# A fused cosine attention and highway layer: q in quads of heads, k left unscaled until the exponential, and a new order of the work

## The chip, the cores and the metric

The kernel runs on one core of a Trainium2 chip. The metric is device time in microseconds (us), the median of several runs. The engines are PE (TensorE; PEld are its weight loads), DVE (VectorE), ACT (ScalarE), POOL (GpSimd) and SP, which only issues transfers here.

## The reference

```python
def _attn_ref(q, k, v, tau):                      # (8, 12, 448, 64) each, tau 0.1
    q_n = q / (np.linalg.norm(q, axis=-1, keepdims=True) + 1e-06)
    k_n = k / (np.linalg.norm(k, axis=-1, keepdims=True) + 1e-06)
    scores = np.matmul(q_n, k_n.transpose(0, 1, 3, 2)) / tau
    attn = np.exp(scores - np.max(scores, axis=-1, keepdims=True))
    attn = attn / (np.sum(attn, axis=-1, keepdims=True) + 1e-09)
    return np.matmul(attn, v)
def _moe_ref(x, w_h, w_t, b_t):                   # x: (3584, 768), w: (768, 768)
    H = np.maximum(x @ w_h, 0.0)
    T = 1.0 / (1.0 + np.exp(-(x @ w_t + b_t)))
    return T * H + (1.0 - T) * x
```

The heads' outputs stand side by side in x: 8 batches of 448 tokens, 768 wide.

## The kernel before

The work goes batch by batch (8), and in a batch by pairs of heads p and p + 6 (6 pairs). The 448 tokens of a head are three chunks of 128 (token 3 l + c on lane l) and a tail of 64.

*Loads.* `load_main` (L361) takes the three chunks of q and k of a batch with one transfer each on POOL's queue, cast to f16 on the way; `load_tails` (L389) takes the tails as f32 on SP's queue; `load_v` (L410) takes v as f32 on SP's queue. Batch 0 comes partly by `load_first` (L377).

*Norms.* `square` (L450) squares q and k on DVE in f16, `folds` (L471) adds halves twice and reduces on DVE; tails are squared on ACT (L487). `newton` (L495) makes 1/norm by two Newton steps, seven small DVE instructions a part.

*Scaling and turning.* `scaled` (L526, the instruction at L532) multiplies q and k of a pair by 1/norm on POOL, giving qn and kp; `qtnorm` (L542) does q's tails on POOL, `ktnorm` (L554, L559) k's tails on DVE into kb. `turn` (L568) transposes on PE, nine 128x128 products a pair, and DVE copies the 1,024 columns to qT (L591).

*Scores.* `scores` (L594) makes, per chunk of k, two products of 64 rows by 448 columns (L600), one for each head, into two PSUM banks, and one exponential of 896 (L607, scale 1/tau) takes both; the tails of k of both heads are one 512-wide product (L614) and exponential (L619). There is no maximum to subtract, since the scores are bounded.

*Attend.* `vcast` and `vtcast` (L623, L632) cast v to f16 on ACT; a 65th column of ones gives the sum of the exponentials. `attend` (L641) gathers 7 groups of 65 columns in one PSUM bank: L648 and L651 for full chunks, L667 for the tail tokens of both heads. DVE takes the reciprocal of the sums (L681) and writes x (L684).

*Highway layer.* `ffn` (L691) runs four times a batch: three groups of 128 tokens over 768 columns, and a tail group whose two column halves stand on the two halves of the lanes. x is transposed (L710) and copied (L715). The bias enters as a product of a row of ones with the bias (L733, tail L730), then come six products of 384 columns per weight and half (L744, tail L739). ACT takes the tanh from PSUM (L758), DVE max(h, 0) - x (L765), the gate (L772) and their product (L776), POOL adds x (L782; in the last two groups DVE), SP stores (L792, tail L790).

*The order.* All this is recorded as some 1,790 operations. The list `ORDER` (L17) puts them in a fixed order; `Plan.follow` (L187) walks the list, gives out buffers by due time and sorts by the start that its own cost figures give. Each engine executes its share in that order. PSUM is two score buffers of two banks (pS) and four banks for all else (pB).

Of the kernel before, what the change touches and what calls it, by code (L numbers as in the profile page):

```python
# [15 lines left out]

ORDER = tuple(  # L17
    int(n)
    for n in """
# [861 lines left out]
```

## Time and profile before

| what | value |
|---|---|
| median of 3 runs | 318.89 us (317.71 to 319.69) |
| span of the profiled execution, first to last instruction | 317.8 us |
| granted TensorE clock, mean | 0.974 of full speed |
| read from HBM, written | 37.75 MB, 11.01 MB |
| first transfer to first exponential of 896 | 20.6 us |
| weights w_h, w_t landed | 34.8, 42.6 us |
| last x written to the end | 25 us |

A group's row in the page reads: line, engine, operation, out<-in, shapes, count, then busy time, mean ns of one, and idle time of the engine just before with what ended it. Recorded durations of neighbours overlap, so the step from one instruction to the next is shorter than a duration. In the slices a digit is the busy share of 1/40 of the span, in tenths.

### The profile page before, as it was taken

How to read it: one execution, taken by the hardware profiler on the slowest of the kernel's cores; microseconds unless marked ns; L12 is line 12 of the kernel's file. 1: busy time of each engine (PE TensorE's matmuls, PEld its weight loads, DVE VectorE, ACT ScalarE, POOL GpSimd, SP SyncE). 2: the span in 40 equal slices, each digit the busy share in tenths (PEclk: the TensorE clock that was granted, in tenths of full speed). 3: DMA queues.
4: the chain of work that ended last, by engine and by line, in shares of the span. 5: the costliest groups of instructions: out<-in, count | busy, mean ns of one | idle time of the engine just before them, and what ended most of it. 6: DMA issues, size and time to landing. Idle time of an engine off the chain costs nothing.

```text
span 317.8 us, 8195 instructions
## 1 busy us (share of the span) xinstructions
PE 272.9 (86%) x3304; PEld 172.9 (54%) x3304; DVE 251.5 (79%) x572; ACT 206.3 (65%) x327; POOL 157.7 (50%) x162
## 2 busy tenths in 40 slices
PE   0167668999899999989999499996999999999992
PEld 0025344665566566555675366573665675666651
DVE  6697794499989987998799969997589686464554
ACT  2348675869789765967777538953699747684120
POOL 9542656243773496277544817349372637010521
PEclk9999995999999999999999989997999999999998
DMA  7999999019921399139811991228911111110304
GB/s 165 254 187 218 228 188 242 14 48 150 228 101 27 105 232 188 28 106 233 153 60 58 146 221 49 71 71 121 273 70 27 49 52 52 28 52 1 123 33 145
DMA packets 62854, 38.09 MB, mean 120 GB/s; under 512 B 43328, under 2 KB 59712, under 8 KB 62816
## 3 DMA queue, kind: packets, MB, share of 16 engines
q1 hardware_dynamic: 36208, 25.47, 29.0%
q0 software_dynamic: 24992, 11.31, 27.6%
q10 hardware_dynamic: 1616, 0.79, 0.9%
q8 instruction: 26, 0.43, 0.5%
q14 instruction: 12, 0.10, 0.1%
HBM read 37.75 MB, written 11.01 MB: 153 GB/s over the span
## 4 chain that ended last, share of the span: by engine, by line
PE 43%; DVE 28%; DMA 11%; issue 9%; POOL 4%; ACT 3%; SPq 1%; POOLq 0%; ACTq 0%; DVEq 0%
PE pB L744 17%; PE pS L600 5%; PE pB L651 4%; DMA kr<-in_k_dram 3%; PE pB L739 3%; DVE f L478 3%; DMA qr<-in_q_dram 3%; DVE sq L463 3%; PE pB L710 3%; DVE hm L765 3%; DVE f L479 2%; DVE n L480 2%; DMA f<-in_k_dram 2%; DMA qt<-in_q_dram 2%; DVE qT L591 2%
## 5 line engine op out<-in xcount | busy, mean ns | idle before, releaser
L607 ACT ACTIVATE E<-pS 128x896 f16<-128x896 f32 x144 | 126.3, 925 | 23.6 <-PE pS L600 22.7
L782 POOL TENSOR_TENSOR os<-x,hm 128x768 f32<-128x768 f16 (+1 forms) x30 | 46.5, 1554 | 84.6 <-DVE hm L776 80.8
L744 PEld LDWEIGHTS <-xT 128*128 128x128 f16 x576 | 52.1, 99 | 36.1 <-issue 10.0
L744 PE MATMUL pB<-wt,xT 128*128 128x384 f16 x288 | 62.3, 331 | 0.1
L744 PE MATMUL pB<-wh,xT 128*128 128x384 f16 x288 | 60.9, 331 | 1.0 <-DVE x L684 0.5
L758 ACT ACTIVATE tt<-pB 128x384 f16<-128x384 f32 x56 | 27.4, 496 | 45.8 <-PE pB L744 35.5
L532 POOL TENSOR_TENSOR kp<-kr,rs 128x384 f16<-128x384 f16 x45 | 40.2, 902 | 29.6 <-DVE rs L513 17.0
L651 PE MATMUL pB<-vp,E 128*128 128x65 f16 x864 | 50.6, 195 | 0.8 <-ACT E L607 0.8
L532 POOL TENSOR_TENSOR qn<-qr,rs 128x384 f16<-128x384 f16 x45 | 39.6, 891 | 22.1 <-PE pB L579 11.0
L765 DVE SCALAR_TENSOR_TENSOR hm<-pB,x 128x384 f16<-128x384 f32 x56 | 30.7, 553 | 23.6 <-PE pB L744 19.9
L600 PE MATMUL pS<-qT 64*128 64x448 f16 x288 | 45.3, 367 | 3.6 <-ACT E L607 3.2
L619 ACT ACTIVATE Et<-pB 128x512 f16<-128x512 f32 x48 | 28.8, 605 | 25.6 <-PE pB L614 22.9
L648 PE MATMUL pB<-vp,Et 128*128 128x65 f16 x288 | 43.9, 194 | 0.5 <-DVE xT L715 0.4
L651 PEld LDWEIGHTS <-E 128*128 128x128 f16 x864 | 40.1, 98 | 5.7 <-ACT E L607 1.3
L591 DVE COPY qT<-pB 128x1024 f16<-128x1024 f16 x48 | 32.3, 682 | 6.9 <-PE pB L585 5.4
L648 PEld LDWEIGHTS <-Et 128*128 128x128 f16 x288 | 28.2, 98 | 9.6 <-issue 6.6
L684 DVE SCALAR_TENSOR_TENSOR x<-pB,rd 128x448 f16<-128x448 f32 x48 | 29.5, 620 | 0.9
L614 PE MATMUL pB<-qT 128*128 128x512 f16 x48 | 19.1, 403 | 4.9 <-DVE qT L591 3.4
L600 PEld LDWEIGHTS <-qT 64*128 64x128 f16 x288 | 10.8, 94 | 21.6 <-issue 16.6
L577 PE MATMUL pB<-ident,qtn 128*128 128x128 f16 x24 | 5.7, 237 | 18.1 <-POOL qtn L545 13.8
L478 DVE TENSOR_TENSOR f<-sq 128x1152 f16<-128x1152 f16 (+2 forms) x25 | 18.4, 746 | 3.3 <-ACT sq L461 3.2
L715 DVE COPY xT<-pB 128x768 f16<-128x768 f16 (+1 forms) x32 | 15.8, 502 | 4.7 <-PE pB L710 4.6
(73 smaller groups left out, 466.1 us busy)
## 6 DMA issues: line engine op xcount, KB each, us to landing
vr<-in_v_dram SPq DMA_DIRECT2D x8, 1152.0 KB, 10.8
out_dram<-os SPq DMA_DIRECT2D x24, 384.0 KB, 2.3
qr<-in_q_dram POOLq DMA_DIRECT2D x7, 576.0 KB, 8.5
kr<-in_k_dram POOLq DMA_DIRECT2D x7, 576.0 KB, 11.6
vt<-in_v_dram SPq DMA_DIRECT2D x16, 96.0 KB, 7.7
out_dram<-os SPq DMA_DIRECT2D x16, 96.0 KB, 2.2
qt<-in_q_dram SPq DMA_DIRECT2D x30, 48.0 KB, 3.8
kt<-in_k_dram SPq DMA_DIRECT2D x14, 96.0 KB, 7.8
```

The source lines that it names most:

```text
L478: lambda: nc.vector.tensor_add(v("f1"), v("sq")[:, :, 0:32], v("sq")[:, :, 32:64]),
L532: e.tensor_mul(R("qn" if t == 0 else "kp", s).rearrange("l c ab d -> l ab c d"), rows(t, b, p, p + 1)[:, :, 0, :].rearrange("l ab (c d) -> ...
L591: op("DVE", f"cpT {s}", lambda: nc.vector.tensor_copy(R("qT", s)[:, :], R16(("T", ti))[:, :]), o, l, key, r=[("B", ("T", ti))], w=[("qT", s)])
L600: nc.tensor.matmul(R("S", 3 * s + c)[:, ab, 0:448], lhsT=qT[:, 512 + 128 * c : 640 + 128 * c], rhs=qT[:, 64 * (1 - ab) : 64 * (1 - ab) + 4 ...
L607: nc.scalar.activation(R("E", s)[:, c, :, 0:448], R("S", 3 * s + c)[:, :, 0:448], AF.Exp, scale=inv_tau)
L619: op("ACT", f"exp {s} t", lambda: nc.scalar.activation(R("Et", s)[:, 64:576], R("B", ("S", s))[:, :], AF.Exp, scale=inv_tau), o, l, key + 0.3,
L648: nc.tensor.matmul(U[:, 2 * c + ab, :], lhsT=Et[:, 128 + 128 * c : 256 + 128 * c], rhs=vp[:, 6 + ab, :], start=True, stop=False)
L651: nc.tensor.matmul(U[:, 2 * c + ab, :], lhsT=EF[:, j, 576 * ab + 128 * c : 576 * ab + 128 * c + 128], rhs=vp[:, 3 * ab + j, :], start=Fals ...
L684: op("DVE", f"ev {s}", lambda: nc.vector.scalar_tensor_tensor(out=R("x", b)[:, :, D * p : D * p + D], in0=U_()[:, :, 0:D], scalar=0.0, in1 ...
L744: nc.tensor.matmul(P[:, 0:MH], lhsT=xT[:, cc, :], rhs=w_[:, cc, MH * mh : MH * mh + MH], start=st, stop=(cc == CC - 1))
L765: nc.vector.scalar_tensor_tensor(out=R("hm", g)[:, MH * mh : MH * mh + MH], in0=R("B", ("P", pi))[:, 0:MH], scalar=0.0, in1=xs, op0=ALU.ma ...
L782: op(en, f"out {g}", lambda: eng.tensor_add(R("os", g)[:, 0:W], xall(), R("hm", g)[:, 0:W]), o, l, at + 0.1, r=[("gg", g), ("x", b)], w=[( ...
```

## The change

The kernel is rewritten in nearly all its parts, for the same tiling over batches, pairs and token groups.

- *q in quads.* q of a batch comes as f32 by two transfers on SP's queue. A lane holds seven consecutive tokens of one head; lanes 0 to 63 hold six heads, lanes 64 to 127 six others. There are no q tails. Three quads of heads a batch: each is scaled by two POOL multiplications of 448, turned by seven products, copied by DVE once (896 columns). The score products now have tokens in the order of lanes, and the groups of attend and x follow it: group j holds tokens 7 l + j.
- *k unscaled.* k is rearranged by two DVE copies a batch (`copy_k`), not multiplied; 1/|k| enters the exponential as its scale, one value per lane. tau goes into q's norm.
- *Norms.* ACT squares q (896 wide) and k (1,152 wide); DVE reduces the squares, f32, without folds. Newton runs over up to 84 columns at once.
- *Exponentials.* One per head and chunk, 448 wide, each from its own bank; 42 a batch, and none of 896 or 512.
- *Attend.* The two products with the tail of k become one of 130 columns; the tail tokens are 64-lane products of half width, eight a pair, each half on its own lanes.
- *v* is cast to f16 by its transfer on POOL's queue; DVE rearranges it; POOL casts the tails of k and v.
- *Bias.* DVE adds it to the projection (f32, into z), tanh reads z, 768 wide from SBUF.
- *PSUM* is one ring of eight single banks.
- *Order.* A new list of 1,879 operations, and `SLOTS`, which names the buffer for each use; `Plan.ordered` follows both as they stand.

Cut to its core:

```diff
-    NR = dict(qr=3, kr=3, qt=2, kt=2, ... E=3, Et=3, rd=2, x=4, xT=3, tt=3, hm=3, os=4, S=2, B=4)
+        qr=(2, [128, 6, 448], FP32), kr=(3, [128, NH, 192], FP16), kt=(2, [128, NP, D], FP32),
...
+        os=(4, [128, DM], FP32), B=(8, [128, 512], FP32))
...
+    def q_src(b, s):
+        return q[b].rearrange("(u s) (l j) d -> s l u (j d)", s=2, j=NJ)[s]
...
+            def fn(eng=eng, src=src, dst=dst):
+                if eng == "ACT":
+                    nc.scalar.activation(dst(), src(), AF.Square, scale=tau)
...
+                nc.vector.reduce_sum(R("n2", b)[:, c : c + 7 * n], s, axis=AX.X)
...
+                a = R("kr", b).rearrange("l (t p) x -> l t p x", t=2)[:, :, p0:p1]
+                nc.scalar.activation(d, a, AF.Square)
...
+                ENG[eng].tensor_mul(
+                    R("qn", 3 * b + g)[:, :, t, :],
+                    R("qr", b)[:, g + 3 * t, :].rearrange("l (j d) -> l j d", d=D),
+                    R("y", b)[:, c : c + 7].unsqueeze(2).to_broadcast([128, NJ, D]))
...
+            for j in range(NJ):
+                nc.tensor.transpose(T[:, j], R("qn", i)[:, j].rearrange("l t d -> l (t d)"), ident[:, :])
...
+    def copy_k(b):
+        for t in range(2):
+            def fn(t=t):
+                nc.vector.tensor_copy(R("kp", b).rearrange("l p c t d -> l (p c) t d")[:, :, t],
+                                      R("kr", b)[:, 6 * t : 6 * t + 6, :].rearrange("l p (c d) -> l (p c) d", c=NC))
...
-                nc.scalar.activation(R("E", s)[:, c, :, 0:448], R("S", 3 * s + c)[:, :, 0:448], AF.Exp, scale=inv_tau)
+                    nc.scalar.activation(R("E", n)[:, at : at + 7, :].rearrange("l j x -> l (j x)"), R("B", ("S", n, c, t))[:, 0:S],
+                                         AF.Exp, scale=R("y", b)[:, col : col + 1])
...
-                    nc.tensor.matmul(U[:, 6, :], lhsT=lt, rhs=rh, start=(n == 0), stop=(n == 7))
+                    lt = E[:, 7 * (2 * m + t) + 6, :] if m < NC else Et[:, 6, :]
+                    nc.tensor.matmul(U[64 * t : 64 * t + 64, 6, :], lhsT=lt, rhs=vp[:, 3 * t + m if m < NC else 6 + t, 0:65],
+                                     start=(m == 0), stop=(m == NC))
...
-                            nc.tensor.matmul(P[:, 0:MH], lhsT=ones[:, :], rhs=bth[:, MH * mh : MH * mh + MH],
-                                             start=True, stop=False)
...
-                        R("tt", g)[:, MH * mh : MH * mh + MH], R("B", ("P", pi))[:, 0:MH], AF.Tanh, scale=0.5),
+                    op("DVE", f"za {g} {mh}", lambda at=at, sl=sl: nc.vector.tensor_add(
+                        R("z", g)[:, sl], R("B", at)[:, 0:MH], biast[:, :] if tail else bias[:, sl]), r=[("B", at), ("b",)], w=[("z", g)])
+                op("ACT", f"th{nb} {g}", lambda: nc.scalar.activation(R("tt", g)[:, 0:W], R("z", g)[:, 0:W], AF.Tanh, scale=0.5),
...
-            for o in plan:
+            for o in pl.ordered(ORDER, SLOTS):
```

More of the change, by code (lines that the diff above doesn't have):

```diff
@@ L170, in begin @@
[L170 to L190 removed]
+                o.deps.update(q for q in writers[t] if q is not o)
@@ L191, in follow, with ordered @@
+    def ordered(self, order, slots):
+        self.link()
+        assert sorted(order) == list(range(len(self.ops)))
+        nth = {n: 0 for n in self.rings}
+        left, held, done = {}, {}, set()
+        for o in self.ops:
+            for t in self.buffers(o):
+                left[t] = left.get(t, 0) + 1
         out = []
-        for n in seqs:
+        for n in order:
             o = self.ops[n]
-            st, take = self.begin(o, free, mode, port)
-            for t, i in take:
-                self.held[t[0]][i] = t
-                self.slot[t] = i
-                if t[0] in self.turns:
-                    self.turns[t[0]].remove(t[1])
-            o.start, o.ready = st, st + o.lat
-            free[o.eng] = st + o.occ
-            if o.port:
-                port = st + o.occ
-            if o.mode is not None:
-                mode = o.mode
-            if o.size:
-                dma = max(dma, st) + o.size / self.BW
-                o.ready = dma + self.LAND
+            assert all(d.seq in done for d in o.deps), o.name
+            for t in self.buffers(o):
+                if t not in self.slot:
+                    i = int(slots[t[0]][nth[t[0]]])
+                    nth[t[0]] += 1
+                    old = held.get((t[0], i))
+                    assert i < self.rings[t[0]] and (old is None or left[old] == 0), (o.name, t, old)
+                    held[t[0], i] = t
+                    self.slot[t] = i
+                left[t] -= 1
+            done.add(n)
@@ L450, in square @@
-    def square(b, p0, p1, key):
-        g0, g1 = 12 * (p0 % 3), 12 * (p0 % 3) + 12 * (p1 - p0)
-        n = 192 * 2 * (p1 - p0)
-        i = (b, p0)
-        for t in range(2):
-            onact = b == 0 and p0 < 3 and (p0 > 0 or t == 0)
-            def fn(t=t, onact=onact):
-                a = rows(t, b, p0, p1)
-                d = R("sq", i)[:, g0:g1, :].rearrange("l (p a c) d -> l a p (c d)", a=4, c=NCH)[:, 2 * t : 2 * t + 2]
-                if onact:
-                    nc.scalar.activation(d, a, AF.Square)
-                else:
-                    nc.vector.tensor_mul(d, a, a)
-            o, l = act(n) if onact else dve(n, 1 if first(b, p0) else 2)
-            op("ACT" if onact else "DVE", f"sq {b} {p0} {t}", fn, o, l, key, r=[rowtok(t, b, p) for p in range(p0, p1)],
-               w=[("sq", i)], port=not onact)
-        folds(f"fold {b} {p0}", b, i, g0, g1, 12 + 12 * p0, [("n2", b, p) for p in range(p0, p1)], key)
@@ L495, in newton @@
-    def newton(b, parts, key):
-        at = [0 if p == 6 else 12 + 12 * p for p in parts]
-        lo, hi = min(at), max(at) + 12
-        assert hi - lo == 12 * len(parts)
-        def step(i):
-            n2 = R("n2", b)[:, lo:hi]
-            y, t, u = (R("rs", b)[:, j, lo:hi] for j in range(3))
+                    h = slice(6 * ab + p0, 6 * ab + p1)
+                    nc.gpsimd.dma_start(d[:, h, :], a[:, h, :])
+        op("POOL", f"ldv {b} {p0}", fn, w=[("vr", b, p) for p in range(p0, p1)])
@@ new lines, in ld_w, with ld_b, fn @@
+    def ld_w(w_src, w_dst, nm):
+        op("POOL", f"ld{nm}", lambda: nc.gpsimd.dma_start(w_dst[:, :, :], w_src.rearrange("(cc p) m -> p cc m", p=128)),
+           w=[(nm,)])
+    def ld_b():
+        def fn():
+            nc.sync.dma_start(bias[:, :], moe_b_t.partition_broadcast(128))
+            for h in range(2):
+                nc.sync.dma_start(biast[64 * h : 64 * h + 64, :],
+                                  moe_b_t[MH * h : MH * h + MH].partition_broadcast(64))
+        op("SP", "ldb", fn, w=[("b",)])
@@ new lines, in norm_t, with newton, step @@
+    def norm_t(b):
+        i, KT = ("t", b), KCS[b > 0][1]
+        op("ACT", f"sqt {b}", lambda: nc.scalar.activation(
+            R("sq", i)[:, 0:384].rearrange("l (p d) -> l p d", d=D), R("kt", b)[:, :, :], AF.Square), r=[("kt", b)], w=[("sq", i)])
+        op("DVE", f"rdt {b}", lambda: nc.vector.reduce_sum(
+            R("n2", b)[:, KT : KT + 6], R("sq", i)[:, 0:384].rearrange("l (g d) -> l g d", d=D), axis=AX.X),
+           r=[("sq", i)], w=[("n2", b, "t")])
+    def newton(b, lo, hi, parts):
+        i = (b, lo)
+        def step(j):
+            n2, y = R("n2", b)[:, lo:hi], R("y", b)[:, lo:hi]
+            t, u = (R("tu", i)[:, m, lo:hi] for m in range(2))
@@ L542, in qtnorm @@
[L542 to L554 removed]
+        for j in range(7):
+            op("DVE", f"nt{hi - lo} {b} {lo} {j}", lambda j=j: step(j), r=[("n2", b) + p for p in parts] if j == 0 else [("nt", i, j - 1)],
+               w=[("nt", i, j)] + ([("y", b) + p for p in parts] if j == 6 else []), u=[("tu", i), ("n2", b), ("y", b)])
@@ new lines, in cast_k0 @@
+    def cast_k0(p, eng):
+        def fn():
+            a = R("os", ("f0", p // 2)).rearrange("l (i h x) -> l i h x", i=2, h=2)[:, p % 2]
+            a, d = a.rearrange("l h (c d) -> l h c d", c=NC), R("kp", 0)[:, p].rearrange("l c t d -> l t c d")
+            ENG[eng].copy(d, a) if eng == "ACT" else ENG[eng].tensor_copy(d, a)
+        op(eng, f"ck {p}", fn, r=[("os", ("f0", p // 2), p)], w=[("kp", 0, p)])
+    def copy_k(b):
[3 more added lines that the diff above has]
+                                      R("kr", b)[:, 6 * t : 6 * t + 6, :].rearrange("l p (c d) -> l (p c) d", c=NC))
+            op("DVE", f"kc {b} {t}", fn, r=[("kr", b, p) for p in range(NP)], w=[("kp", b, p) for p in range(NP)])
@@ L695, in ffn @@
+    def ffn(b, i):
         g = 4 * b + i
@@ L698, in ffn @@
         nb = 3 if tail else 6
+        T = "t" if tail else ""
         def xcols(j):
@@ L779, in ffn @@
-        last = b == B - 1 and i >= 2
-        eng, en = (nc.vector, "DVE") if last else (nc.gpsimd, "POOL")
-        o, l = dve(W) if last else pool(W)
-        op(en, f"out {g}", lambda: eng.tensor_add(R("os", g)[:, 0:W], xall(), R("hm", g)[:, 0:W]), o, l, at + 0.1,
-           r=[("gg", g), ("x", b)], w=[("os", g)], u=[("hm", g)], port=True)
-        def store():
-            rows = out[b * S : b * S + S]
-            O = R("os", g)
-            if tail:
-                for h in range(2):
-                    nc.sync.dma_start(rows[384:448, MH * h : MH * h + MH], O[64 * h : 64 * h + 64, 0:MH])
-            else:
-                nc.sync.dma_start(rows[0:384].rearrange("(l c) m -> l c m", c=NCH)[:, i, :], O[:, :])
@@ new lines, in ffn @@
+        eng = "DVE" if b == B - 1 and i >= 2 else "POOL"
+        for mh in range(1 if tail else 2):
+            sl = slice(MH * mh, MH * mh + MH)
+            op(eng, f"out {g} {mh}", lambda sl=sl, mh=mh: ENG[eng].tensor_add(R("os", g)[:, sl], xpart(mh), R("hm", g)[:, sl]),
+               r=[("gg", g), ("x", b)], w=[("os", g)], u=[("hm", g)])
+        def store():
+            rows, O = out[b * S : b * S + S].rearrange("(l j) m -> j l m", j=NJ), R("os", g)
+            for h in range(2):
+                if tail:
+                    nc.sync.dma_start(rows[6, :, MH * h : MH * h + MH], O[64 * h : 64 * h + 64, 0:MH])
+                else:
+                    nc.sync.dma_start(rows[2 * i + h], O[64 * h : 64 * h + 64, :])
@@ new lines, in ffn @@
+        op("SP", f"st {g}", store, r=[("os", g)], w=[("o", g)])
+    for b in range(B):
+        if b == 0:
+            ld_q(0, [0], "SP")
+            ld_k0(0, "ACT")
+            ld_kt(0, "ACT")
+            ld_k0(1, "ACT")
+            ld_q(0, [1], "SP")
+            for p in range(2, 6):
+                ld_k0(p, "SP")
+            ld_q(0, [2], "SP")
+            ld_v(0, 0, 3)
+            ld_v(0, 3, 6)
+            ld_vt(0)
+            ld_w(moe_w_t, wt, "wt")
+            ld_w(moe_w_h, wh, "wh")
+            ld_b()
+            norm_q(0, 0, True)
+            newton(0, 0, 14, [("q", 0)])
+            norm_k(0, 0, 1)
+            norm_t(0)
+            newton(0, 14, 26, [("k", 0), ("t",)])
+            norm_k(0, 1, 3)
+            newton(0, 26, 38, [("k", 1), ("k", 2)])
+            norm_q(0, 1, False)
+            norm_q(0, 2, False)
+            newton(0, 38, 66, [("q", 1), ("q", 2)])
+            norm_k(0, 3, 6)
+            newton(0, 66, 84, [("k", 3), ("k", 4), ("k", 5)])
+            for p in range(NP):
+                cast_k0(p, "DVE")
+        else:
+            ld_q(b)
+            ld_k(b)
+            ld_kt(b, "SP")
+            ld_v(b)
+            ld_vt(b)
+            norm_q(b, 0, False)
+            norm_k(b, 0, 3)
+            norm_t(b)
+            if b == 1:
+                newton(b, 0, 38, [("q", 0), ("k", 0), ("k", 1), ("k", 2), ("t",)])
+            norm_q(b, 1, False)
+            norm_q(b, 2, False)
+            norm_k(b, 3, 6)
+            if b == 1:
+                newton(b, 38, 84, [("q", 1), ("q", 2), ("k", 3), ("k", 4), ("k", 5)])
+            else:
+                newton(b, 0, 84, [("q", g) for g in range(3)] + [("k", p) for p in range(6)] + [("t",)])
+            copy_k(b)
+        cast_kb(b, "POOL")
+        if b == 0:
+            copy_v(b, 0, 3)
+            copy_v(b, 3, 6)
+        else:
+            copy_v(b, 0, 6)
+        cast_vt(b, "POOL")
+        for g in range(NG):
+            first = b == 0 and g == 0
+            scale_q(b, g, ("DVE", "POOL") if first else ("POOL", "POOL"))
+            turn_q(b, g, 2 if first else 1)
+            turn_k(b, g, b > 0)
+        for p in range(NP):
+            scores(b, p)
+            attend(b, p)
@@ L838 @@
         for i in range(4):
-            ffn(b, i, base + 6 + OFF + i * 8 * 6 / 28)
-    plan = pl.follow(ORDER)
-    with nc.allow_low_precision(reason="fp16 operands of the products, squares and gates as given"):
+            ffn(b, i)
+    with nc.allow_low_precision(reason="fp16 operands of the products and gates as given"):
         with tc.manual_schedule():
-            for o in plan:
+            for o in pl.ordered(ORDER, SLOTS):
                 o.fn()
```

731 lines of the change are left out of this document (264 added, 467 removed), and 144 rows, old and new, of the table ORDER.

## The prediction, made before the result was known

> **What bounds the kernel now.** I read the page first: totals, slices, chain.
>
> ```profile
> PE 272.9 (86%) x3304; PEld 172.9 (54%) x3304; DVE 251.5 (79%) x572; ACT 206.3 (65%) x327; POOL 157.7 (50%) x162
> PE   0167668999899999989999499996999999999992
> DVE  6697794499989987998799969997589686464554
> DMA  7999999019921399139811991228911111110304
> PE 43%; DVE 28%; DMA 11%; issue 9%; POOL 4%; ACT 3%; SPq 1%; POOLq 0%; ACTq 0%; DVEq 0%
> ```
>
> No engine is full on average. PE is short of work for the first six slices of 7.9 us, while the DMA engines are full; from then on it stands at 9 nearly throughout, with DVE close behind. The chain that ended last alternates between these two (43% and 28%).
>
> Next the windows, cut where the first score product of each batch starts (19.95, 50.34, ... us).
>
> ```profile
> 0.00:19.95 19.95, 2.04 (x10) 0.90 (x11) 13.43 (x58) 4.21 (x6) 12.79 (x21) 1.00 1.08 206
> 19.95:50.34 30.39, 21.67 (x295) 13.32 (x296) 26.45 (x62) 21.61 (x33) 15.60 (x18) 0.97 1.27 204
> 50.34:84.21 33.87, 32.35 (x374) 19.99 (x374) 25.59 (x58) 26.98 (x44) 15.53 (x17) 0.93 0.70 126
> 84.21:116.96 32.75, 32.32 (x418) 21.13 (x419) 29.87 (x68) 25.98 (x42) 19.55 (x20) 1.00 0.42 116
> 116.96:149.10 32.14, 29.71 (x365) 18.57 (x363) 29.22 (x62) 23.12 (x35) 19.92 (x22) 1.00 0.67 143
> 149.10:191.50 42.40, 37.38 (x463) 24.18 (x463) 36.39 (x73) 27.39 (x44) 20.12 (x20) 0.96 0.72 128
> 191.50:229.74 38.24, 35.65 (x431) 22.50 (x429) 32.68 (x70) 26.58 (x44) 21.01 (x20) 0.96 0.54 115
> 229.74:263.08 33.34, 32.93 (x425) 21.45 (x423) 28.42 (x66) 25.31 (x40) 18.75 (x19) 1.00 0.15 54
> 263.08:317.80 54.72, 48.82 (x537) 30.84 (x536) 29.46 (x62) 25.13 (x39) 14.41 (x11) 0.97 0.18 63
> ```
>
> Columns: stretch, length, busy PE, PEld, DVE, ACT, POOL, clock, DMA. So there are four parts: a start of 20.0 us, batch 0 in 30.4, six steady stages of 35.4 on average (212.7 in all), and an end of 54.7. In the steady stages DVE is busy 30.4 us each (86%), ACT 25.9.
>
> Busy PE time holds the overlap of neighbours, so I take the step from one instruction to the next, from the timeline, with durations from the groups.
>
> ```profile
> 155.74 1.72 ACT L607 ACTIVATE E<-pS 128x896 f16<-128x896 f32 x2
> 303.98 1.63 PE L744 MATMUL pB<-wt,xT 128*128 128x384 f16 x9
> 152.16 0.26 PE L667 MATMUL pB<-vp,E 128*128 128x65 f16 x3
> 311.25 0.66 PE L739 MATMUL pB<-wh,xT 128*64 128x384 f16 x6
> L607 ACT ACTIVATE E<-pS 128x896 f16<-128x896 f32 x144 | 126.3, 925 | 23.6 <-PE pS L600 22.7
> L667 PE MATMUL pB<-vp,E 128*128 128x65 f16 x288 | 18.2, 194 | 0.1
> L744 PE MATMUL pB<-wt,xT 128*128 128x384 f16 x288 | 62.3, 331 | 0.1
> L765 DVE SCALAR_TENSOR_TENSOR hm<-pB,x 128x384 f16<-128x384 f32 x56 | 30.7, 553 | 23.6 <-PE pB L744 19.9
> L480 DVE TENSOR_REDUCE n<-f 128x36 f32<-128x576 f16 x15 | 11.0, 740 | 0.0
> ```
>
> Nine full products of 384 columns take 1.63 us, so a step is (1.63 - 0.33) / 8 = 0.162; a 65-column one (0.26 - 0.19) / 2 = 0.033; six of the half-width products 0.66, three pairs, so 0.08 each. Six x transposes took 0.51, a step of 0.056. Two exponentials took 1.72, so neighbours overlap by 0.12. Changing between row-tiled, column-tiled and full products adds some 0.09 (0.126 instead of 0.033 from an attend product to a score one).
>
> **The change, per batch.** PE in steps, before: projections 72 x 0.162 + 24 x 0.08 = 13.6; bias products 6 x 0.162 + 2 x 0.08 = 1.1; turns 54 + 21 x transposes at 0.056 = 4.2; scores 18 pairs of 0.19 = 3.5; six 512-wide 0.227 = 1.4; attend 192 x 0.032 = 6.1: 29.9 us. The order changes tiling 182 times, 23 a batch: 2.1. So PE needs 32.0 of 35.4.
>
> After: no bias products (-1.1); 21 + 24 turns instead of 54 (-0.5); the tail score product 448 wide instead of 512 (-0.2); two Et products merged into one 130 wide (two steps of 0.03 against one of about 0.057: nothing); the attend tail as 48 half-width products that write the two partition halves, in pairs as line 739 runs, 0.016 instead of 0.032 each (-0.8). Sum -2.6. The new order changes tiling 175 times, as many. PE: 29.3. The tail is the uncertain one: half-width weight loads last 110 ns here against 98 full ones, so if pairs do not run beside each other it saves nothing (-1.8 in all), or if each load is waited for it costs 48 x (0.11 - 0.03) = +3.8. I take the pairing, since line 739 is the same form with longer rows. The Trainium skill (TensorEngine Tiling (Array Packing), "Gotcha 2: Feature Incompatibilities") says that column tiling excludes Fast Weight Load; by it the tail keeps its old price, and the total would be about 5 us longer.
>
> DVE, recorded means. Removed: squares 2 x (0.947 + 0.793), folds 2 x (0.864 + 0.695) + 0.572 + 0.25, reductions 2 x 0.740 + 0.344, 14 Newton steps of 0.31, two kb products of 0.735 (they go to POOL, as casts), six qT copies of 0.682: 19.2. Added: reductions of unfolded squares, by the row's slope (740 for 576, 344 for 192: 1.03 ns an element) 3 x 1.07 + 2 x 1.33 + 0.54 = 6.4; seven wider Newton steps of 0.36; three qT copies of 0.62 and three kT copies of 0.68; seven bias additions, priced as line 765, PSUM in and 384 wide, 0.553 = 3.9; two k and two v rearrangements of 1,152 elements. Those four have no row: the nearest is the gate's 768-wide f16 tensor_scalar, 0.36 undisturbed, which gives 0.46 each, 1.8; at the reduction's one element a step they cost 1.33 each, 5.3. Sum 18.5 to 22.0; five instructions fewer overlap, +0.4. So DVE changes by -0.3 to +3.2; I take 0, near the copy row, and keep 30.4.
>
> ACT: the v casts go (8 x 0.52 = -4.2) and the qt squares (-0.5); q squares 3 x 0.94, k squares 2 x 1.15 come (768 wide took 0.834; +5.1). 42 exponentials of 448, by the rows of 384 and 512 (496, 605) 0.55 each, 23.1, replace 18 x 0.925 + 6 x 0.605 = 20.3. Tanh 3 x 0.83 + 0.5 instead of 7 x 0.496: -0.5. Together +2.7, less 11 more overlaps of 0.12: +1.4, so 27.3. The exponential's scale is now a column per partition, which no row has: it costs from nothing up to the whole overlap, 0.12 x 42 = 5.0; I take nothing, nearest to the rows.
>
> POOL: six q products of 448 (two elements a ns as at 384 and 768: 0.95 each) and four small casts instead of 13 products of 0.9: about 3 us less; its 18 to 21 of 35 hide that. Transfers: q goes from POOL's queue to SP's, in rows of seven tokens and without the tail loads; v goes from SP's to POOL's. On SP, q stands behind stores that wait for POOL's sums (193 us of waits there now), but k's and v's tails already stood there, a batch ahead. I cost that at nothing; the cover is that lead, and a missed one would cost a landing, 8 to 12 us once.
>
> **The sum, on the profiled span of 317.8.** Start: the first exponential comes at 20.6 now, after k normalisation and casts of k that wait for Newton; after, k needs only a cast before its transposes. From landings at about 8 (the first q now lands at 7.3), DVE's work ahead of it (two reductions and q's scaling at 0.55, Newton 1.5, copies 1) ends near 15, exponential near 16: -4 (-6 to +1). Batch 0: bound by loads at 204 GB/s and the norms of batch 1; fewer small rows: -3 (-6 to 0). Six steady stages: PE leads the chain and DVE at 30.4 still fits: -2.6 each, -15.6, a period of 32.8. End: PE has 46.2 us in the old order after that point and 42.9 in the new one: -3.3. Together -25.9: 291.9. The span is 1.1 under the median of the runs, 318.89, so **293 us**, 283 to 303 for this case alone.
>
> **The rivals.**
> *Tighter order.* PE now loses 3.4 us a stage beyond its own work. If the new order loses 1.4, the period is 30.7: -28, and with -6 in batch 0 277 us. For it: ten changes of a pace-setting engine go into one order that also interleaves Newton chains. Against it: DVE at 30.4 would have to be 99% busy.
> *ACT becomes the bound.* If exponentials with a column scale do not overlap, ACT has 32.3; at PE's 93% that is a period of 34.8: -3.6 instead of -15.6, 305 us. The Trainium skill (ScalarE: Activation LUTs, "What ACT_TABLE_LOAD costs") gives 93 ns for each per-partition pointer; an estimate by it is 3.9 us a batch, and 299 us. No run so far shows such an instruction.
> *DVE paces already.* Its 86% holds, its work stays, the period stays 35.4; start, batch 0 and end alone give 309; nearly even if the start gains nothing.
> *DVE paces and gets more (slower).* With the rearrangements at one element a step DVE has 33.6; at its 86% the period is 39.1: +22 instead of -15.6, 331 us. For it: DVE is 28% of the chain, and three f32 reductions and seven additions are new. Against it: waits on PE end much of its idle time (19.9 us at line 765). It decides from DVE 31.5 on, where six stages give back the other savings.
>
> **How the numbers follow.** Forecast 0.42, tighter 0.17, ACT 0.12, DVE as now 0.09, DVE worse 0.20. The range 270 to 326 leaves out 0.03 below and 0.14 above. A measurement of this kernel tells about 1% from no change. Faster by over 1%: 0.42 + 0.17 + 0.12 + 0.03 of the fourth = 0.74; within 1%: 0.06 of the fourth + 0.02 of the last = 0.08; slower 0.18.
>
> **What would show it.** First exponential near 16; stages near 32.8 with DVE under 31 busy; exponentials of 0.55 that start 0.43 apart; attend tails of 0.13 for eight products; rearrangements of 0.46. Wrong if exponentials stand 0.5 apart with ACT over 90%, if the rearrangements take over 1 us, or if PE waits for q loads behind stores.

## The result, and the profile after

| | median | runs | ratio to before, 95% interval |
|---|---|---|---|
| before, run beside it | 319.29 us | 317.71 to 322.36 (4) | |
| after | 290.19 us | 289.75 to 291.58 (4) | 0.9122 [0.907, 0.9174] |

The profiled execution of the kernel after took 289.78 us, of which 288.0 are the span; the granted clock was 0.995 of full speed (0.974 before). The median of four lies 0.4 us above that execution. Experiments e4 and e7 had slow runs, which their ratios leave out and their medians do not.

The totals, two rows of slices and the chain, from the profile of the kernel after:

```profile
PE 255.9 (89%) x3024; PEld 160.7 (56%) x3024; DVE 241.1 (84%) x544; ACT 242.5 (84%) x421; POOL 130.3 (45%) x166
DVE  2896895479999899999979999799999878565994
ACT  3378999999799989999999997989999787894220
PE 38%; ACT 35%; DMA 8%; DVE 8%; issue 4%; SPq 2%; POOL 2%; POOLq 0%; ACTq 0%; DVEq 0%
ACT E L514 25%; PE B L593 15%; PE B L508 5%; PE B L538 5%; DMA qr<-in_q_dram 5%; ACT Et L521 5%; PE B L590 3%; DMA kt<-in_k_dram 2%; PE B L546 2%; ACT sq L353 2%; ACT tt L609 2%; POOL os L619 2%; PE B L533 2%; PE B L431 2%; PE B L577 1%
```

The chain has changed hands: DVE stood for 28% of it and has 8%, ACT for 3% and has 35%, a quarter of the whole in the exponentials of line 514. ACT's busy time rose by 36 us while the span fell by 30.

The windows, cut as those shown of before at the first score product of each batch (stretch, length, busy PE, PEld, DVE, ACT, POOL with counts, clock, DMA share, GB/s):

```profile
0.00:16.02 16.02, 1.51 (x12) 1.18 (x12) 9.56 (x33) 5.83 (x9) 7.83 (x18) 1.00 1.00 200
16.02:44.87 28.85, 23.06 (x230) 12.54 (x230) 24.32 (x70) 26.70 (x47) 14.00 (x21) 1.00 1.24 235
44.87:78.84 33.97, 32.50 (x405) 20.22 (x403) 25.53 (x54) 32.51 (x56) 13.28 (x18) 1.00 1.09 166
78.84:110.64 31.80, 30.94 (x372) 19.26 (x370) 29.57 (x63) 30.24 (x53) 18.63 (x22) 1.00 0.93 161
110.64:141.65 31.01, 30.33 (x381) 19.32 (x379) 30.08 (x63) 30.99 (x54) 14.36 (x19) 1.00 0.56 106
141.65:174.07 32.42, 31.66 (x401) 20.43 (x398) 29.72 (x66) 30.52 (x53) 16.72 (x20) 1.00 0.75 129
174.07:205.74 31.67, 30.91 (x381) 19.94 (x379) 29.86 (x62) 30.17 (x53) 15.24 (x20) 1.00 0.62 132
205.74:235.14 29.40, 28.87 (x353) 18.60 (x352) 25.30 (x55) 26.95 (x49) 14.55 (x18) 1.00 0.29 49
235.14:288.00 52.86, 46.10 (x512) 29.25 (x507) 37.14 (x85) 28.56 (x51) 15.71 (x18) 0.97 0.34 91
```

In the six steady stages ACT is now busy 30.2 us of 31.7 (95%; 73% before) and 100% of the fifth row. The gain lies thus: start 3.9, batch 0 1.5, steady stages 22.4, end 1.9 us, together 29.8. And it is not spread over the stages: row by row the six gain -0.1, 1.0, 1.1, 10.0, 6.6 and 3.9. Two stages of before, 42.4 and 38.2 us long, hold 16.6 of the 22.4. They also held more matmuls than the others (463 and 431 records of 3,304 in all; the same rows after have 401 and 381 of 3,024), so a part of the unevenness is only where the old order put its work.

In those two PE's idle time (length less busy PE) fell from 7.6 to 1.5 us, and the clock rose from 0.96 to 1.00; the rest of the 16.6 us is busy time of PE. The idle time of before is mostly two waits for DVE's eviction of x, the instruction of line 684 that reads x from PSUM and so frees the bank. The two, from the waits of PE before between 149 and 232 us, then the longest row of after between 141 and 206 us (us in total, times, longest):

```profile
PE pB L577 <- DVE x L684: 3.9, 1, 3.9
PE pB L710 <- DVE x L684: 2.4, 1, 2.4
```

```profile
PE B L593 <- ACT E L514: 0.3, 2, 0.2
```

The longer one can be read at 176 us. First DVE, then POOL, then PE of the kernel before in the same microseconds (start, length, line, count, and in brackets the idle time before with what ended it), then windows there:

```profile
175.82 0.68 DVE L591 COPY qT<-pB 128x1024 f16<-128x1024 f16 x1
176.42 4.09 DVE L479 TENSOR_TENSOR f<-f 128x576 f16<-128x576 f16 x1
180.43 0.19 DVE L681 RECIPROCAL rd<-pB 128x7 f32<-128x7 f32 x1
```

```profile
176.21 0.85 POOL L545 TENSOR_TENSOR qtn<-qt,rs 128x384 f16<-128x384 f32 x1
177.00 2.40 POOL L532 TENSOR_TENSOR kp<-kr,rs 128x384 f16<-128x384 f16 x3
179.37 1.82 POOL L532 TENSOR_TENSOR qn<-qr,rs 128x384 f16<-128x384 f16 x2
```

```profile
178.00 0.36 PE L600 MATMUL pS<-qT 64*128 64x448 f16 x2
182.23 0.27 PE L577 MATMUL pB<-ident,qtn 128*128 128x128 f16 x1 [3.87 <-DVE x L684]
```

```profile
174.00:178.00 4.00, 3.80 (x57) 2.61 (x56) 3.97 (x4) 3.45 (x6) 3.99 (x6) 1.00 0.68 89
178.00:182.20 4.20, 0.37 (x5) 0.19 (x3) 4.20 (x7) 1.54 (x2) 3.19 (x4) 0.94 1.51 186
182.20:184.20 2.00, 1.97 (x13) 1.45 (x13) 1.97 (x5) 0.00 (x0) 0.00 (x0) 0.50 1.41 178
184.20:186.20 2.00, 2.00 (x19) 1.16 (x18) 1.22 (x2) 0.00 (x0) 0.00 (x0) 0.78 1.31 240
```

A fold whose median is 0.45 us lasts 4.09, while POOL multiplies without a pause. Of the fifteen folds of this shape, it is the only one over 0.48. DVE's eviction of x stands behind it, PE waits 3.87 us for that, and then has a clock of 0.50 for two microseconds and of 0.78 for two more. Nothing in the totals shows this: the fold counts as busy DVE, the slow products as busy PE.

To size such stretching, I took for every shape on DVE the tenth percentile of its durations, and summed what the others lie above it: 38.0 us before, 11.6 after. Evictions from PSUM and reductions add next to nothing to it; the operations from SBUF tiles to SBUF tiles make it up. Counted instead: 50 DVE instructions before and 13 after last over 1.5 times their shape's tenth percentile. Each of them overlaps work of POOL (products, sums, casts or the issue of a transfer), none reads PSUM, and none is a reduction.

### The profile page after: what moved, and what is told of

It reads as the page before. It is cut to its first block, busy times and chain, and to the rows that moved or that the text cites. A ratio compares the mean times of both kernels' runs of the same rounds, so it can differ in the third digit from the quotient of the medians.

```text
span 288.0 us, 7655 instructions
## 1 busy us (share of the span) xinstructions
PE 255.9 (89%) x3024; PEld 160.7 (56%) x3024; DVE 241.1 (84%) x544; ACT 242.5 (84%) x421; POOL 130.3 (45%) x166
## 4 chain that ended last, share of the span: by engine, by line
PE 38%; ACT 35%; DMA 8%; DVE 8%; issue 4%; SPq 2%; POOL 2%; POOLq 0%; ACTq 0%; DVEq 0%
ACT E L514 25%; PE B L593 15%; PE B L508 5%; PE B L538 5%; DMA qr<-in_q_dram 5%; ACT Et L521 5%; PE B L590 3%; DMA kt<-in_k_dram 2%; PE B L546 2%; ACT sq L353 2%; ACT tt L609 2%; POOL os L619 2%; PE B L533 2%; PE B L431 2%; PE B L577 1%
## 5 line engine op out<-in xcount | busy, mean ns | idle before, releaser
L514 ACT ACTIVATE E<-B,y 128x448 f16<-128x448 f32 x288 | 163.2, 690 | 12.3 <-PE B L508 12.0
L619 POOL TENSOR_TENSOR os<-x,hm 128x384 f32<-128x384 f16 x53 | 48.6, 929 | 87.3 <-DVE hm L614 60.6
L419 POOL TENSOR_TENSOR qn<-qr,y 128x448 f16<-128x448 f32 x47 | 44.3, 960 | 49.8 <-DVE y L408 30.7
L593 PE MATMUL B<-wt,xT 128*128 128x384 f16 x288 | 57.6, 326 | 0.7 <-DVE xT L579 0.3
L593 PE MATMUL B<-wh,xT 128*128 128x384 f16 x288 | 57.3, 326 | 0.8 <-ACT E L514 0.3
L508 PE MATMUL B<-qT,kT 64*128 64x448 f16 x288 | 49.3, 369 | 6.6 <-ACT Et L521 2.3
L538 PE MATMUL B<-vp,E 128*128 128x65 f16 x864 | 44.9, 194 | 0.1
L605 DVE SCALAR_TENSOR_TENSOR hm<-B,x 128x384 f16<-128x384 f32 x56 | 29.9, 547 | 5.8 <-PE B L593 3.7
L533 PE MATMUL B<-vp,Et 128*128 128x130 f16 x144 | 32.3, 224 | 0.5 <-ACT Et L521 0.2
L521 ACT ACTIVATE Et<-B,y 128x448 f16<-128x448 f32 x48 | 31.9, 686 | 0.1
L554 DVE SCALAR_TENSOR_TENSOR x<-B,rd 128x448 f16<-128x448 f32 x48 | 29.3, 617 | 0.8
L458 DVE COPY kT<-B 128x1024 f16<-128x1024 f16 (+1 forms) x27 | 16.6, 619 | 2.8 <-PE B L452 2.8
```

The costliest lines, as they stand in the source:

```text
L419: ENG[eng].tensor_mul(R("qn", 3 * b + g)[:, :, t, :], R("qr", b)[:, g + 3 * t, :].rearrange("l (j d) -> l j d", d=D), R("y", b)[:, c : c + ...
L508: nc.tensor.matmul(R("B", ("S", n, c, t))[:, 0:S], lhsT=R("kT", i)[ln, s, 128 * c : 128 * c + 128], rhs=R("qT", i)[ln, s, :], start=True, ...
L514: nc.scalar.activation(R("E", n)[:, at : at + 7, :].rearrange("l j x -> l (j x)"), R("B", ("S", n, c, t))[:, 0:S], AF.Exp, scale=R("y", b) ...
L521: op("ACT", f"expt {n}", lambda: nc.scalar.activation(R("Et", n).rearrange("l j x -> l (j x)"), R("B", ("St", n))[:, 0:S], AF.Exp, scale=R ...
L533: nc.tensor.matmul(U[:, 2 * c : 2 * c + 2, :], lhsT=Et[:, 2 * c : 2 * c + 2, :].rearrange("l j x -> l (j x)"), rhs=vp[:, 6:8, 0:65], start ...
L538: nc.tensor.matmul(U[:, 2 * c + t, :], lhsT=E[:, at : at + 2, :].rearrange("l j x -> l (j x)"), rhs=vp[:, 3 * t + m, 0:65], start=False, s ...
```

## The experiments

All ratios are to the kernel before, run on the same chip beside it; the kernel after has 0.912.

**e1, a constant scale.** In the kernel after, both exponentials:

```diff
-  AF.Exp, scale=R("y", b)[:, col : col + 1])
+  AF.Exp, scale=1.25)
```

> The changed kernel with an immediate scale of 1.25 in all exponentials instead of one value per lane; 1/|k| is left out of the scores. Theory (ACT paces the steady stages, since the exponentials now start 0.516 us apart and not 0.43): the step falls to 0.43, ACT loses 0.086 x 42 = 3.6 us a batch, and PE with its own 29.3 us a batch takes over: stages of 30.5 instead of 31.7, batch 0 shorter by 1 to 2; in all 281 us, ratio to the kernel before 0.88. Rival (PE alone paces, ACT is only busy beside it): the step falls too, but the time stays within 2 us of 290, ratio 0.905 to 0.912.

279.32 us, 0.8747 [0.8715, 0.8779]: ScalarE sets the pace, with TensorE close behind it, since of some 31 us taken from the exponentials 11 come off the time. The kernel after shows no wait for 1/|k| before them, so it is the scale and not the lost dependence. The exponentials of the kernel after, then of e1 (busy us, mean ns):

```profile
L514 ACT ACTIVATE E<-B,y 128x448 f16<-128x448 f32 x288 | 163.2, 690 | 12.3 <-PE B L508 12.0
```

```profile
L514 ACT ACTIVATE E<-B 128x448 f16<-128x448 f32 x288 | 136.5, 564 | 23.8 <-PE B L508 22.2
```

From start to start of neighbours it is 0.516 us with the scale by lane and 0.424 with a constant: 0.092 for the scale by lane, 42 times a batch, 3.9 us. ACT's idle time before the exponentials doubles: it waits for PE again.

**e2, PE work added.** The bias products of before, as products with a zero tile, ahead of each projection with w_t in the kernel after (cut):

```diff
+                    bz = w_ is wt
+                    if bz and lo == 0:
+                        for h in range(2 if tail else 1):
+                            nc.tensor.matmul(P[64 * h : 64 * h + 64, 0:MH] if tail else P[:, 0:MH],
+                                             lhsT=ident[:, 0:64] if tail else ident[:, :], rhs=nil[:, :], start=True, stop=False)
```

> The changed kernel with the bias products put back on PE, on a tile of zeros, while DVE still adds the bias: 48 products of 0.162 us and 8 pairs of 0.16, 9.1 us of PE in all, 1.1 a batch. Theory (ACT paces): PE goes from 29.3 to 30.4 a batch and stays under 31.7; in the end part, where ACT is only half busy, it costs its share of about 1.7; in all +2 to +4, 293 us, ratio 0.92. Rival (PE paces): nearly all of it shows, +8 to +9, 298 us, ratio 0.937.

293.18 us, 0.9191 [0.9155, 0.9228]: 2 to 3 us for 9 us of PE's steps (6.8 us of busy time). TensorE follows close behind ACT, but does not set the pace.

**e3, DVE work taken.** The kernel after, with reductions over half of the squares, so that the norms are estimates (the line for q; those of k are shortened the same way):

```diff
-  nc.vector.reduce_sum(R("n2", b)[:, c : c + 7 * n], s, axis=AX.X)
+  nc.vector.reduce_sum(R("n2", b)[:, c : c + 7 * n], s[:, :, 0:32], axis=AX.X)
```

> The changed kernel with DVE reducing only 32 of the 64 squares of each token (the norms are then estimates from half of the elements): 2.9 us of DVE less a batch, 22 in all. Theory (ACT and PE pace, DVE keeps up): 288 to 290 us, ratio 0.905 to 0.912; what is gained comes from the start, where the reductions stand ahead of the first score, at most 1.5 us. Rival (DVE paces, or shares the pace, being busy for 30 of 31.7 us): 280 us or less, ratio under 0.88.

288.73 us, 0.9047 [0.9019, 0.9075]: DVE's busy time fell from 241.1 to 222.8 us and brought some 2 us at most. It does not pace the kernel after.

**e4, PE work taken from the kernel before.** No bias products:

```diff
-  if wi == 0 and lo == 0:
+  if False:
...
-  st = cc == 0 and wi == 1
+  st = cc == 0
```

> The kernel before with the bias products left out (the bias is then missing): 9.1 us of PE less, 1.1 a batch. Theory of the forecast (PE led the old chain, one for one): -8 to -9 us, ratio 0.972 to 0.975. Rival (DVE, held up by POOL, paced the old kernel as much as PE did): -1 to -4 us, ratio 0.987 to 0.997.

316.43 us, 0.9877 [0.9813, 0.9942]: 2 to 6 us for 9 us of steps (6.3 of busy time). PE's time did not pass one for one in the old order.

**e5, DVE work taken from the kernel before.** No folds; the exponentials' constant scale is 64 times smaller, so that they stay bounded.

```diff
-  lambda: nc.vector.tensor_add(v("f1"), v("sq")[:, :, 0:32], v("sq")[:, :, 32:64]),
-  lambda: nc.vector.tensor_add(v("f2"), v("f1")[:, :, 0:16], v("f1")[:, :, 16:32]),
-  lambda: nc.vector.reduce_sum(R("n2", b)[:, to : to + g1 - g0], v("f2"), axis=AX.X),
+  lambda: None,
+  lambda: None,
+  lambda: nc.vector.reduce_sum(R("n2", b)[:, to : to + g1 - g0], v("sq")[:, :, 0:16], axis=AX.X),
```

> The kernel before without its two fold adds (lines 478 and 479, 18.4 and 12.5 us of VectorE in the profile before, 3.9 us a batch); the reduction then takes 16 of the 64 squares of a group, so its length is that of before and the norms are left wrong. Theory A, VectorE set the old pace: most of the 31 us comes off, 291 to 299 us. Theory B, the old order and its handoffs set it and no engine alone: 0 to 6 us, 313 to 319 us.

313.82 us, 0.9819 [0.975, 0.9887]. DVE is busy 20 us less and the kernel is 4 to 8 us shorter. DVE's work by its amount did not set the old pace either. The stretching stays (34.8 us by the sum above): other operations take it over.

**e6, POOL's products taken from the kernel before.** Same instructions, one element each, for all pairs behind the third (cut; the two inputs are shortened like the output):

```diff
+  n = 1 if s > 2 else D
-  R("qn" if t == 0 else "kp", s).rearrange("l c ab d -> l ab c d"),
+  R("qn" if t == 0 else "kp", s).rearrange("l c ab d -> l ab c d")[:, 0 : 2 if s < 3 else 1, 0 : NCH if s < 3 else 1, 0:n],
...
```

> The kernel before with GpSimd's scalings of q and k (line 532, 45 times 0.90 us each, 80 us) cut to one element for all pairs behind the third; the scores of those pairs are then made from older rows. VectorE's instructions are the same ones, but the 38 us by which they are stretched while GpSimd works should mostly go. Theory A, VectorE set the old pace and was stretched by GpSimd: 20 to 30 us off, 289 to 299 us. Theory B, order and handoffs: 0 to 6 us off, 313 to 319 us.

303.81 us, 0.9538 [0.9479, 0.9597]: half of the change's gain, without touching the instructions of PE, DVE or ACT. It lies between the two theories' ranges. The fold of line 479 in the profile before, then in e6 (durations: least, median, most):

```profile
L479 DVE TENSOR_TENSOR f<-f x25: 244/447/4090, 8.8 to 252.2; 128x576 f16<-128x576 f16 x15, 128x192 f16<-128x192 f16 x9, 128x384 f16<-128x384 f16 x1
```

```profile
L479 DVE TENSOR_TENSOR f<-f x25: 244/448/477, 8.2 to 235.4; 128x576 f16<-128x576 f16 x15, 128x192 f16<-128x192 f16 x9, 128x384 f16<-128x384 f16 x1
```

The median has not moved, the tail is gone; the stretching over all of DVE is 20.3 us instead of 38.0 (20 instructions over 1.5 times instead of 50) and the clock 0.991. The chain of e6 (before it was PE 43%, DVE 28%, POOL 4%):

```profile
PE 65%; DVE 17%; DMA 8%; ACT 5%; issue 3%; POOL 0%; SPq 0%; POOLq 0%; DVEq 0%; ACTq 0%
```

POOL's own 4% are gone too, so e6 does not separate the stretching of DVE from POOL's products being late; both go with the 60 us that POOL is busy less. For the stretching speaks that in the six steady stages of the profile before no wait of PE, DVE or ACT is put down to POOL, while PE's longest waits there, 3.9 and 2.4 us, are for DVE. That is an argument, not a test.

**e7, all three.** e4, e5 and e6 in one kernel. The bias, the norms' full sums and most scalings are left out.

> The kernel before with all three at once: no bias products on TensorE (9 us), no folds on VectorE (31 us), GpSimd's scalings cut to one element (80 us). Left out: the bias, the norms' full sums and the scaling of most pairs. If the engines took turns as the bound, each hidden behind the next, the three together give much more than their sum alone: 280 us or less. If the old order itself held the stages at 35 us, the three together give under 15 us: over 304 us.

301.57 us, 0.9383 [0.9291, 0.9475]: 17 to 23 us, between the two expectations, and some 5 us more than e6 alone (from nothing to 10 by the two intervals). PE is busy 260.7 us and DVE 215.4, less than in e6 by 6 and 19. The stages still take 33.5 us on average, from 29.8 to 40.1, by the first exponentials of the profiled execution, which took 302.33 us. So with POOL out of the way, neither engine's work shortens the old kernel much. That its order holds the stages is what remains; no run changed the old order alone.

**e9, the list of banks.** The kernel after with its order, but for each PSUM tile the bank that has been free longest in that order:

```diff
-  i = int(slots[t[0]][nth[t[0]]])
+  i = free[t[0]].pop(0)
```

> The kernel after with its order unchanged on every engine, but each PSUM tile given the bank that has been free longest in that order, in place of the list of banks written into the kernel (474 of the tiles sit elsewhere). Nothing is left out. If the list carries part of the gain, and its lack is what hurt the scaled-k run, 300 us or more. If any bank of the ring of eight does as well, 288 to 293 us.

296.12 us, 0.9266 [0.9208, 0.9323]: some 5 us over the kernel after, from between the two ranges. The list written into the kernel is worth that much, not more.

**e8, e10, e12: 1/|k| into k, for a better kernel.** e1 leaves 11 us to be had, so three kernels multiply k by 1/|k| ahead of its turns and give the exponentials a constant scale: in e8 all pairs of batches 1 to 7, ahead of the first k turn and with banks as in e9; in e10 pairs 2 to 5 and in e12 pairs 4 and 5 of batches 2 to 7, with the banks and the order kept. Cut, from e10, where the engine of the first product is DVE:

```diff
+  ENG[eng].tensor_mul(R("kp", b)[:, p].rearrange("l c t d -> l t c d"),
+                      R("kr", b).rearrange("l (t p) (c d) -> l p t c d", t=2, c=NC)[:, p],
+                      R("y", b)[:, a : a + 6].rearrange("l (t c) -> l t c", t=2).unsqueeze(3).to_broadcast([128, 2, NC, D]))
...
+  nc.gpsimd.tensor_mul(R("kb", b)[ln, 2:6, ab, :], R("kt", b)[ln, 2:6, :],
+                       R("y", b)[ln, KCS[1][1] + 2 : KCS[1][1] + 6].unsqueeze(2).to_broadcast([64, NP - 2, D]))
...
-  AF.Exp, scale=R("y", b)[:, col : col + 1])
+  AF.Exp, scale=1.0 if b > 1 and p > 1 else R("y", b)[:, col : col + 1])
```

> The kernel after with 1/|k| multiplied into k by VectorE (four products of 576 elements in place of two copies of 1152, about 1.3 us more a batch) and into the tail rows by GpSimd, for the batches behind the first; their exponentials take an immediate scale. Nothing is left out. In the constant-scale run an exponential took 0.424 us start to start against 0.516 with the scale by lane: 42 of them a batch give ScalarE 3.9 us back, and PE and VectorE stand ready at about 29.5 and 30 us a batch. Theory, ScalarE paces the kernel after: 280 to 286 us. Rival, the longer VectorE work and the later k turns give it back: 288 us or more.

> The kernel after, banks and order kept, with 1/|k| multiplied into k of pairs 2 to 5 in batches 2 to 7 by VectorE (four products of 384 elements a batch, queued behind the batch's first k turn) and into their tail rows by GpSimd; 28 exponentials a batch then take an immediate scale. Nothing is left out. Theory, ScalarE paces the kernel after: 28 times 0.092 us times six batches is 15 us off ScalarE, of which VectorE's products (some 0.5 us each, less the shorter copies) may take a third back: 276 to 285 us. Rival, VectorE has no room for them at the stage's boundary, as in the scaled-k run: 289 us or more.

> As the late-k run, but for pairs 4 and 5 alone: two products of 384 elements a batch, queued behind the batch's second k turn, so away from the stage's boundary; 14 exponentials of batches 2 to 7 take an immediate scale. Nothing is left out. ScalarE loses 14 times 0.092 us times six, 7.7 us. Theory, ScalarE paces and VectorE has room away from the boundary: 283 to 288 us. Rival, VectorE has no room anywhere while GpSimd's products stretch its own (0.80 us each in the late-k run, where some 0.45 would be undisturbed): 290 us or more, half of the late-k run's loss or so, 293 to 296 us.

e8 takes 325.18 us, 1.0201 [1.0147, 1.0255]; e10 299.5 us, 0.9352 [0.9291, 0.9413]; e12 294.91 us, 0.9256 [0.9221, 0.929]. All three are slower than the kernel after, as the rivals said, but e12 shows a cause that neither theory had named. From first exponential to first exponential its stages of batches 1 to 6 take 32.6, 32.1, 36.1, 32.5, 32.0, 29.3 us, against 32.6, 31.8, 31.3, 32.4, 31.4, 29.5 after: of 7.3 us that its span is longer, 4.8 lie in one stage, and 2.3 before batch 1, which the edit doesn't touch. The profiled execution is 2.1 us above e12's median, so it shows one such stage and not how often it comes. SP's queue, of the kernel after and of e12 (queue and line, what it waited for, us in total, times, longest):

```profile
SPq L628 <- POOL os L619: 104.5, 11, 23.0
SPq L302 <- POOL vp L495: 8.1, 1, 8.1
```

```profile
SPq L728 <- POOL os L719: 84.7, 8, 21.7
SPq L384 <- POOL kb L570: 69.9, 4, 26.4
```

and e12's chain at the start of its long stage (start, length, what):

```profile
112.31 1.56 SPq L384
113.92 0.62 SPq L728
114.58 2.78 DMA out_dram<-os
117.52 0.91 POOL os L719
...
119.28 1.16 POOL qn L501
120.49 0.92 PE B L513 x7
```

Line 384 (line 302 in the kernel after) loads the tail of k. With the products, POOL reads the tail only behind Newton, so its buffer comes free later; the next load of it waits at the head of SP's queue, 18.2 us here; the stores behind it (line 728) wait too; POOL runs out of output tiles and stands 5.5 us; its scaling of q (line 501), queued behind, is late, and so are PE's q turns. The two products added to a batch also cost DVE 0.70 us each (0.80 in e10; 1.20 in e8, where they are of 576 elements). The same waits at line 384 are 68.9 us in e10, and 67.7 us in e8 at its line 374. How much of e10 and e8 is the one and how much the other stays open. A version that leaves the tail with its scale by lane, and so its buffer as it was, wasn't tried.

**e11, one square of q on POOL.** In the kernel after, batches 1 to 7:

```diff
-  eng = "DVE" if t == 1 else "ACT"
+  eng = "DVE" if t == 1 else "POOL" if b > 0 and g == 2 else "ACT"
```

> The kernel after with one of the three squares of q in each batch behind the first made by GpSimd in place of ScalarE (896 elements, some 2 us of GpSimd a batch), and one 14-element scaling on VectorE for it. Nothing is left out. Theory, ScalarE paces the kernel after: 0.84 us a batch off ScalarE, 284 to 288 us. Rival, GpSimd makes it late or stretches VectorE's copies and gives it back: 290 us or more.

292.46 us, 0.9149 [0.91, 0.9199]. ACT is busy 4.8 us less and nothing is won: the rival. DVE's stretching rose from 11.6 to 14.8 us and POOL waits for q and v's tails before the square (6.8 us in two waits). So no kernel here beats the one after with the whole computation in it.

## Where the prediction held and where it failed, point by point

The time was within 3 us of the forecast, but the sum got there with one term too small and two too large, and one of the prediction's own signs of being wrong came true: exponentials that stand 0.5 apart (0.516) with ACT over 90% (95% in the steady stages). That the total fits is partly luck. With a constant scale, which is what the forecast's price of nothing amounts to, the kernel takes 279.3 us (e1), 14 under the forecast: a cost and a gain that it had both left out stood against each other.

*Start, batch 0, end* (-4, -3, -3.3): measured -3.9, -1.5, -1.9. The start is right, with its first exponential at 16.6 us (forecast: near 16). The end's step, that PE's shorter work passes whole, gave a little over half.

*Six stages at -2.6 each* (-15.6): measured -3.7 each on average, -22.4. The step that failed is "PE leads the chain and DVE at 30.4 still fits: -2.6 each". Busy PE per stage went from 33.4 to 30.9, as sized, but that is a weak sign, since busy time isn't work: e1 runs the same 3,024 products with 247.7 us of busy PE in place of 255.9. And PE's work doesn't pass one for one. e4 took 9 us of PE's steps from the old kernel and e2 added as many to the new one, and the time moved by 2 to 6 and 2 to 3 us. At e4's rate the 21 us of steps that the forecast takes from PE (8 x 2.6) would be worth 5 to 14 us, an estimate.

What went besides are stalls like that at 176 us: in the six stages PE's idle time fell from 12.4 to 5.1 us, and four waits over 0.8 us, each behind a stretched DVE instruction, became none. Taking 60 us from POOL is worth about 15 us in the old kernel (e6); the change takes 27. e7 leaves POOL and DVE less busy than the kernel after does (96.6 and 215.4 us against 130.3 and 241.1), though PE not, and still stands some 8 us above it by the ratios. So about that much came with the new kernel's order, its layout and the rest of PE's shorter work, the start's 4 among it. The list of banks is worth about 5 in the new kernel (e9). What else in the order carries the rest was not separated.

*POOL, "about 3 us less" a batch, hidden.* This is the term that was costed at nothing and was not: POOL's busy time fell by 27 us. Its own share of the old chain was 4%, but DVE's operations between SBUF tiles were stretched beside it. ("Two elements a ns" should read two ns an element; the 0.95 us of a product is right, 0.96 measured.) The old profile had the stretching in plain sight: the prediction priced the fold of line 479 at its mean, 0.695, over a median of 0.45. The Trainium skill (SBUF — State Buffer, "Who interferes with whom") says that a DVE instruction with two SBUF inputs contends with a GpSimd instruction that reads SBUF, and that one with at most one SBUF input outside the two-port modes doesn't. The traces agree: 4.09 us for the fold during POOL's products, at most 0.48 without them (e6), and no eviction from PSUM at line 684 over 0.63 with or without. Copies with one SBUF input are stretched too (line 485 of the kernel after, 0.45 us to 1.80); no run here shows in which mode they ran, nor how the two engines are arbitrated.

*ACT: "it costs from nothing up to the whole overlap, I take nothing".* The wrong end was taken: 0.092 us an exponential, 3.9 a batch. The Trainium skill (ScalarE: Activation LUTs, "What ACT_TABLE_LOAD costs") gives 93 ns for a per-partition pointer, and e1 against after agrees within 1 ns. So the rival's mechanism came true, ACT is the bound, but not its time of 305: it let ACT reach only "PE's 93%" and added to ACT a full 5.0, whereas ACT is busy 92 to 100% of its stages. (The 93% follows from no row: busy PE was 94% of the old stages, and the prediction's own 32.0 of 35.4 are 90%. By the rival's own sum 3.9 us would give some 297 us, not 299.) 42 steps of 0.516, with the squares and tanh, come to 29.3, recorded as 30.2, and the period is 31.7. That an engine can be busy throughout a stage needs the others to be ready for it; what in the new order does this was not tested.

*DVE: taken 0, up to +3.2.* Busy DVE fell by 2.0 a stage (30.4 to 28.3). The prices were right: the rearrangements step at 0.37 us and last 0.45 undisturbed (forecast 0.46; 0.55 and 0.62 as recorded means, stretched), the bias additions 0.548 (0.553), the reductions 1.07 and 1.34 (1.07 and 1.33). The slower rival fell with them. The difference has the size of the stretching: in the six stages it fell from 31 to 9 us, 3.7 a stage, so DVE's undisturbed work rose by some 1.7, inside the forecast's range.

*Attend tails.* Eight half-width products step in 0.13 us, as forecast:

```profile
36.39 0.28 PE L546 MATMUL B<-vp,E 128*64 128x65 f16 x6
36.51 0.20 PE L546 MATMUL B<-vp,Et 128*64 128x65 f16 x2
```

From the Trainium skill (TensorEngine Tiling (Array Packing), "Gotcha 2: Feature Incompatibilities"), which says that column tiling excludes Fast Weight Load, the prediction drew that they could keep the old price. The trace doesn't show that: the loads are longer, 111 and 114 ns against 98, but lie beside other products.

*Loads.* "If PE waits for q loads behind stores" did not happen in the steady stages of the kernel after, where PE waits for nothing over 0.4 us. In e12 PE did wait for late q, 3.7 us for its scaling, by a longer way round than the forecast had, and one stage became 4.8 us longer.

## What to carry to other kernels

Read durations by their spread, not their mean: a row whose median is 0.45 and whose longest is 4.09 us points at an engine that takes something from it, and one such instruction in front of an eviction stopped TensorE for 3.87 us and then lowered its clock. Before work goes from a full engine to an idle one, ask what it shares with its neighbour, and when its inputs' buffers come free, for a load that waits for a buffer also held the stores queued behind it in e12. And give each step its own test: here a total within 1% hid two errors that cancelled.

## What the runs showed of the hardware

- A scale by lane costs an exponential from PSUM 0.092 us against a constant (0.516 and 0.424 from start to start, 448 wide).
- A DVE operation between SBUF tiles was stretched ninefold (0.45 to 4.09 us) while six POOL products ran, and those took their usual 0.8 to 0.9 us each.
- After a wait of 3.87 us PE was granted 0.50 and then 0.78 of its clock in the next four microseconds; over the whole span the clock went with the stalls: 0.974 before, 0.991 with POOL relieved, 0.995 after.
